# Weight preparation, gating and chunk decays issued in another order in a fused retention and SwiGLU kernel

## The chip, the cores and the metric

One Trainium2 chip, one core. The metric is device microseconds of one execution; lower is better. Three runs of the kernel before gave 822.98, 823.74 and 824.34 us.

## What is computed

A retention block feeds a SwiGLU feed-forward block. Queries, keys and values have shape (4, 8, 768, 64) in float32; the weights are (512, 1536), (512, 1536) and (1536, 512) and arrive as float64.

```python
for t in range(S):                                   # each batch and head
    state = gamma * state + outer(k[t], v[t])
    y[t] = q[t] @ state / sqrt(D)
x = y.transpose(0, 2, 1, 3).reshape(B * S, H * D)    # 3072 x 512
g = x @ w_gate
out = (g * sigmoid(g) * (x @ w_val)) @ w_out
```

## The kernel before

**Stages.** The 24 chunks of 128 positions (6 for each of 4 batches) are worked off in 4 segments of 6 chunks. The first stage is the retention of segment 0. Then, in each segment, `up` runs for 12 blocks f = 0 to 11 (columns of the two first weights), and `down` for 3 parts u. Between the products of `down` the steps of the next segment's retention are dealt out one by one, so that after the first stage retention has no stage of its own.

**Retention of a chunk.** `scores` multiplies k and q (PE) and masks the result out of PSUM (DVE); POOL makes a decayed copy of q (`qd`, L253) and of k (`kd`, L257). `mix` adds the old state's part and the masked part into the PSUM bank y, of which there is one, and ScalarE (ACT) copies it to xT. `state` multiplies `kd` with v and DVE scales the old state (L279) and adds (L280). After every second chunk DVE makes the sums `xs` (L334 to L337).

**A block of up.** Seven products, a Strassen-like scheme with 7 in place of 8, each of two float32 matmuls (four records in the profile), in this order: B11, T1, T2, B22, T3, B21, T4. B11, T2, T3 and T4 go through the bank x, T1 and B22 through w, B21 through z. ACT copies x after B11 (p, L359), w after T1 (p, L362) and x after T2 (u, L368); DVE adds after B22 (L370) and after T3 (L372), and adds z to the first copy (c, L377). ACT takes the silu of c (L378) and of x after T4 (sg, L381), and DVE multiplies both into hT (L382, L383). PE may not go on into a bank before it was read: T2 waits for the copy of L359, T3 for L368, T4 for the sum of L372.

**Weights.** In segment 0 each piece (12 `up`, 6 `down`) is turned from float64 words to float32: two ACT operations (`convert_a`), two tensor-scalar operations on DVE (`convert_b`), one combined operation on DVE (L188) and an integer add on POOL (L190). Then three operations make the sums that the scheme needs (L198 to L200): on POOL for `up`, on DVE for `down`. Finished `up` pieces are written to DRAM and read back in the later segments. There are three raw buffers, and the next load is issued on SP when a piece leaves its buffer. The table `at_block` says which pieces block f prepares: `up` f + 2, and in every even block the `down` piece f // 2 too.

**What sets the order.** Every engine runs its own instructions in the order in which the program issues them; nothing reorders them (`manual_schedule`). `retain(n)` issues n steps of the first retention, and `convert(f, 0)` and `convert(f, 1)` issue a block's preparation at two places in `up`. The list `late` holds the multiplications of a block, which are issued after T1 of the next.

Of the kernel before, what the change touches and what calls it, by code (L numbers as in the profile page):

```python
# [10 lines left out]
F32 = mybir.dt.float32  # L11
# [3 lines left out]
ALU = mybir.AluOpType  # L15
# [22 lines left out]
def tile_retnet_swiglu(  # L38
# [53 lines left out]

    def load_chunk(c, pool, tag):
        tiles = []
        for nm, src in (("kt", k_t), ("qt", q_t), ("kn", k_n), ("vn", v_n)):
            t = pool.tile([P, 512], F32, tag=nm + tag, name=f"{nm}_{c}")
            nc.sync.dma_start(out=t, in_=src[c])
            tiles.append(t)
        chunks[c] = tiles

# [81 lines left out]
    def convert_c(piece):  # L182

        kind, a = piece
        if piece in raw:
            w, d, lo, hi = words_of(piece)
            u = d.bitcast(U32)
            nc.vector.scalar_tensor_tensor(u, u, 3, hi, op0=ALU.logical_shift_left,  # L188
                                           op1=ALU.bitwise_xor)
            nc.gpsimd.tensor_tensor(d.bitcast(I32), u.bitcast(I32), lo.bitcast(I32),  # L190
                                    op=ALU.add)
            del raw[piece]
        w = wt[0, a] if kind == "up" else wot[a]
        sub = (nc.gpsimd if kind == "up" else nc.vector).tensor_tensor
# [6 lines left out]
        if kind == "up":  # L201
# [3 lines left out]

    at_block = [[("up", f + 2)] * (f + 2 < NF) + [("down", f // 2)] * (f % 2 == 0)
                for f in range(NF)]
    order = [("up", 0), ("up", 1)] + sum(at_block, [])
# [28 lines left out]
    def scores(c):  # L237
# [8 lines left out]
        for i in range(2):  # L246
            t = mid.tile([P, NP, P], F32, tag=f"a{i}", name=f"a{i}_{c}")
            nc.vector.tensor_tensor(t, pairs(sp[i]), mask[:, i], op=ALU.mult)  # L248
            a.append(t)
        att[c] = a  # L250
        if c % NCK:
            qd = mid.tile([P, NP, P], F32, tag="qd", name=f"qd_{c}", bufs=1)
            nc.gpsimd.tensor_tensor(qd, qt, qdec, op=ALU.mult)  # L253
            att[c, "qd"] = qd
        if c % NCK < NCK - 1:
            kd = mid.tile([P, H, D], F32, tag="kd", name=f"kd_{c}", bufs=1)
            nc.gpsimd.tensor_tensor(  # L257
                kd, chunks[c][2].rearrange("p (h d) -> p h d", h=H),
                kdec[:, :, None].to_broadcast([P, H, D]), op=ALU.mult)
            att[c, "kd"] = kd  # L260

    def state(c):
        ci = c % NCK
        if ci == NCK - 1:
            return
        kd = att.pop((c, "kd"))
        vn = chunks[c][3]
        st = bank("st", 1, f"st_{c}")
        for n in range(NP):
            nc.tensor.matmul(st[:, ts(n, P)], kd[:, ds(2 * n, 2)], vn[:, ts(n, P)],  # L270
                             start=(n == 0), stop=True, skip_group_check=True)
        new, old = state_of(c), state_of(c, 1)
        for i in range(2):
# [3 lines left out]
            else:  # L277
                g = gdec[r, :, None].to_broadcast([D, NP, D])
                nc.vector.tensor_tensor(new[r, :, r], old[r, :, r], g, op=ALU.mult)  # L279
                nc.vector.tensor_tensor(new[r, :, r], new[r, :, r],  # L280
                                        pairs(st)[r, :, r], op=ALU.add)

    def mix(c):
        ci = c % NCK
        vn = chunks[c][3]
        a = att.pop(c)
        y = bank("y", 1, f"y_{c}")
        if ci:
            qd = att.pop((c, "qd"))
            prev = state_of(c, 1)  # L290
# [50 lines left out]
    def up(s, f, convert):  # L341
# [20 lines left out]
        nc.scalar.copy(p5, wb)  # L362
        while late:
            late.pop(0)()
        convert(f, 0)
# [5 lines left out]
        product(x, T3, s3, start=False)  # L371
        tt(hT[:, f, 1], x, p5, op=add)  # L372
        convert(f, 1)
        z = bank("wz", 2, f"z_{s}_{f}")[:, :TH]
        product(z, B21, a_up(0, 1))
        c11 = tmp("c11", 2)
        tt(c11, z, p1, op=add)  # L377
        nc.scalar.activation(c11, c11, AF.Silu)  # L378
        product(x, T4, a_up(1, 1), start=False)
        sg = tmp("sg", 1)  # L380
        nc.scalar.activation(sg, x, AF.Silu)  # L381
        late.append(lambda: tt(hT[:, f, 0], hT[:, f, 0], c11, op=mul))  # L382
        late.append(lambda: tt(hT[:, f, 1], hT[:, f, 1], sg, op=mul))  # L383

# [63 lines left out]


    cs = seg_chunks(0)  # L450
    load_chunk(cs[0], first, "0")
    nc.scalar.dma_start(out=tab, in_=decays)
    for n in range(1, len(cs)):
        load_chunk(cs[n], first, str(n))
        if n in (2, 3, 4):
            load_next()
# [6 lines left out]

    retain(8)
    for p in order[:2]:
        convert_a(p)
        retain(2)
        convert_b(p)
        retain(2)
        convert_c(p)  # L470
        load_next()
    for p in at_block[0]:
        convert_a(p)
    retain(len(steps))
    early.__exit__(None, None, None)
    hp = ctx.enter_context(tc.tile_pool(name="hp", bufs=1))
    hT = hp.tile([P, NF, 2, TH], F32, name="hT")

    def convert(f, part):
        now = at_block[f]  # L480
        if part == 0:
            for p in now:
                convert_b(p)
            for p in now[:1]:
                convert_c(p)
                load_next()
        else:
            for p in now[1:]:
                convert_c(p)
                load_next()  # L490
            if f + 1 < NF:
                for p in at_block[f + 1]:
                    convert_a(p)

# [72 lines left out]
```

## Time and profile before

| what | value |
|---|---|
| median of 3 runs | 823.74 us |
| profiled execution | 824.35 us |
| its span, first to last instruction | 822.6 us |
| around the span | 1.75 us |
| PE (matmul) busy | 764.5 us, 93% of the span |
| DVE busy | 342.9 us, 42% |
| ACT busy | 190.7 us, 23% |
| POOL busy | 132.1 us, 16% |

A busy share is a mean over stages that are unlike each other; the rows further down tell the stages apart. Mean duration and idle time of a group of instructions stand in one row, with what ended the idle time.

### The profile page before, as it was taken

How to read it: one execution, taken by the hardware profiler on the slowest of the kernel's cores; microseconds unless marked ns; L12 is line 12 of the kernel's file. 1: busy time of each engine (PE TensorE's matmuls, PEld its weight loads, DVE VectorE, ACT ScalarE, POOL GpSimd, SP SyncE). 2: the span in 40 equal slices, each digit the busy share in tenths (PEclk: the TensorE clock that was granted, in tenths of full speed). 3: DMA queues.
4: the chain of work that ended last, by engine and by line, in shares of the span. 5: the costliest groups of instructions: out<-in, count | busy, mean ns of one | idle time of the engine just before them, and what ended most of it. 6: DMA issues, size and time to landing. Idle time of an engine off the chain costs nothing.

```text
span 822.6 us, 8808 instructions
## 1 busy us (share of the span) xinstructions
PE 764.5 (93%) x3440; PEld 535.8 (65%) x3440; DVE 342.9 (42%) x556; ACT 190.7 (23%) x358; POOL 132.1 (16%) x102
## 2 busy tenths in 40 slices
PE   6566779779999999999999999999999999999997
PEld 5443445445888755555888855555888855555886
DVE  3975555645536133233626333323555123322520
ACT  2333334432010123222110122222110122222100
POOL 3735556352111000000111100010111000000000
PEclk9978899889999999999999999999999999999999
DMA  9645655733245022340245022340254122220010
GB/s 335 209 147 180 210 174 179 229 126 117 90 167 180 26 90 100 124 147 1 90 167 179 27 89 90 112 169 0 69 188 146 59 90 90 89 90 0 1 41 37
DMA packets 40697, 95.74 MB, mean 116 GB/s; under 512 B 3664, under 2 KB 15952, under 8 KB 40656
## 3 DMA queue, kind: packets, MB, share of 16 engines
q1 hardware_dynamic: 37056, 88.09, 30.9%
q10 hardware_dynamic: 3600, 7.09, 2.5%
q8 instruction: 27, 0.44, 0.2%
q14 instruction: 14, 0.11, 0.0%
HBM read 77.86 MB, written 17.30 MB: 116 GB/s over the span
## 4 chain that ended last, share of the span: by engine, by line
PE 77%; DVE 1%; POOL 0%; ACT 0%; issue 0%; DVEq 0%; ACTq 0%; POOLq 0%
PE x L349 24%; PE dx L408 15%; PE w L349 12%; PE dw L408 8%; PE z L349 6%; PE dz L408 4%; PE s L243 2%; PE y L296 2%; PE y L292 2%; PE st L270 2%; POOL wot L190 0%; DVE wot L198 0%; DVE wot L188 0%; ACT sg L381 0%; DVE wot L199 0%
## 5 line engine op out<-in xcount | busy, mean ns | idle before, releaser
L349 PE MATMUL x<-xs,wt 128*128 128x384 f32 x384 | 147.3, 508 | 28.2 <-ACT p L359 28.2
L349 PE MATMUL w<-xs,wt 128*128 128x384 f32 x384 | 144.0, 499 | 0.6 <-DVE xs L334 0.6
L349 PE MATMUL x<-xT,wt 128*128 128x384 f32 x384 | 132.4, 486 | 1.1 <-DVE hT L372 1.1
L349 PEld LDWEIGHTS x<-xs,wt 128*128 128x128 f32 x384 | 75.8, 199 | 83.4 <-issue 35.2
L349 PEld LDWEIGHTS w<-xs,wt 128*128 128x128 f32 x384 | 75.3, 196 | 54.7 <-issue 5.2
L349 PEld LDWEIGHTS x<-xT,wt 128*128 128x128 f32 x384 | 72.8, 190 | 51.4 <-issue 1.7
L370 DVE TENSOR_TENSOR hT<-w,u 128x384 f32<-128x384 f32 x48 | 26.8, 558 | 168.9 <-PE w L349 163.0
L349 PE MATMUL z<-xT,wt 128*128 128x384 f32 x192 | 69.8, 486 | 0.0
L378 ACT ACTIVATE c<-c 128x384 f32<-128x384 f32 x48 | 25.1, 522 | 186.9 <-DVE c L377 186.9
L408 PE MATMUL dw<-wot,hs 128*128 128x256 f32 x288 | 67.3, 383 | 0.0
L253 POOL TENSOR_TENSOR qd<-qt,tab 128x512 f32<-128x512 f32 x20 | 27.4, 1369 | 247.8 <-PE y L292 120.5
L408 PE MATMUL dx<-wot,hs 128*128 128x256 f32 x288 | 67.0, 382 | 0.0
L408 PE MATMUL dx<-wot,hT 128*128 128x256 f32 x288 | 66.4, 381 | 0.0
L408 PEld LDWEIGHTS dw<-wot,hs 128*128 128x128 f32 x288 | 53.7, 190 | 8.7 <-issue 1.5
L408 PEld LDWEIGHTS dx<-wot,hT 128*128 128x128 f32 x288 | 53.7, 190 | 8.6 <-issue 1.0
L408 PEld LDWEIGHTS dx<-wot,hs 128*128 128x128 f32 x288 | 53.4, 190 | 7.7
L349 PEld LDWEIGHTS z<-xT,wt 128*128 128x128 f32 x192 | 36.5, 190 | 25.4
L257 POOL TENSOR_TENSOR kd<-kn,tab 128x512 f32<-128x512 f32 x20 | 21.9, 1093 | 187.1 <-DMA kn<-in_k_n_dram 96.5
L299 ACT COPY xT<-y 128x512 f32<-128x512 f32 x24 | 14.0, 584 | 150.3 <-PE y L296 150.2
L248 DVE TENSOR_TENSOR a<-s,tab 128x512 f32<-128x512 f32 x48 | 30.8, 684 | 40.6 <-PE s L243 40.6
L280 DVE TENSOR_TENSOR state<-state,st 64x256 f32<-64x256 f32 x32 | 13.4, 418 | 67.2 <-PE st L270 66.3
L243 PE MATMUL s<-qt,kt 64*128 64x128 f32 x384 | 30.3, 298 | 11.7 <-DMA qt<-in_q_t_dram 8.3
(58 smaller groups left out, 745.0 us busy)
## 6 DMA issues: line engine op xcount, KB each, us to landing
wt<-wstore SPq DMA_DIRECT2D x36, 896.0 KB, 4.6
wstore<-wt SPq DMA_DIRECT2D x12, 896.0 KB, 4.8
kt<-in_k_t_dram SPq DMA_DIRECT2D x24, 256.0 KB, 4.9
qt<-in_q_t_dram SPq DMA_DIRECT2D x24, 256.0 KB, 5.1
kn<-in_k_n_dram SPq DMA_DIRECT2D x24, 256.0 KB, 5.3
vn<-in_v_n_dram SPq DMA_DIRECT2D x24, 256.0 KB, 4.4
raw_up<-in_w_val_dram SPq DMA_DIRECT2D x24, 256.0 KB, 5.5
raw_up<-in_w_gate_dram SPq DMA_DIRECT2D x12, 512.0 KB, 6.0
```

The source lines that it names most:

```text
L243: nc.tensor.matmul(sp[i][:, ts(n, P)], kt[r, n], qt[r, n], start=True, stop=True, skip_group_check=True)
L248: nc.vector.tensor_tensor(t, pairs(sp[i]), mask[:, i], op=ALU.mult)
L253: nc.gpsimd.tensor_tensor(qd, qt, qdec, op=ALU.mult)
L257: nc.gpsimd.tensor_tensor(kd, chunks[c][2].rearrange("p (h d) -> p h d", h=H), kdec[:, :, None].to_broadcast([P, H, D]), op=ALU.mult)
L270: nc.tensor.matmul(st[:, ts(n, P)], kd[:, ds(2 * n, 2)], vn[:, ts(n, P)], start=(n == 0), stop=True, skip_group_check=True)
L292: nc.tensor.matmul(y[:, ts(n, P)], prev[:, n], qd[:, n], start=(n == 0), stop=False, skip_group_check=True)
L296: nc.tensor.matmul(y[ds(D * i, D), ts(n, P)], vn[:, ts(2 * n + i, D)], a[i][:, n], start=(ci == 0 and n == 0), stop=True, skip_group_check ...
L299: nc.scalar.copy(xT[:, :, c // NCK % 2, ts(ci % L, P)], pairs(y))
L349: nc.tensor.matmul(o, w[:, slot, k], a[:, k], start=(start and k == 0), stop=(stop and k == KH - 1), skip_group_check=True)
L370: tt(hT[:, f, 0], wb, u2, op=add)
L378: nc.scalar.activation(c11, c11, AF.Silu)
L408: nc.tensor.matmul(o, a[:, k], wot[k][:, slot], start=(start and k == 0), stop=(k == FH - 1), skip_group_check=True)
```

## The change

Six things change. (1) The three sums of a weight piece become a step of their own, `sums_t`. For the two pieces that the first stage converts, and for every `down` piece, it is issued later: at the start of the next block, from the list `due`. (2) The `down` pieces move from the even blocks to the odd ones (the last to block 10), and the first block's conversion is issued after the retention, not inside it. (3) The two silus of a block are issued on ACT after the second copy of the next block, and the two multiplications after that block's L372. (4) k and q are scaled in place, k first, where there were copies of their own. (5) The old state is scaled by ACT, in four operations of 128 columns, ahead of the products; DVE only adds. (6) The decay table is loaded in two parts on SP between the first chunk's tensors, v is loaded ahead of k, and the first weight piece is loaded one chunk earlier.

```diff
-        for nm, src in (("kt", k_t), ("qt", q_t), ("kn", k_n), ("vn", v_n)):
+        for nm, src in (("kt", k_t), ("qt", q_t), ("vn", v_n), ("kn", k_n)):
             t = pool.tile([P, 512], F32, tag=nm + tag, name=f"{nm}_{c}")
             nc.sync.dma_start(out=t, in_=src[c])
             tiles.append(t)
+            between(nm)
...
                                     op=ALU.add)
             del raw[piece]
+
+    def sums_t(piece):
+        kind, a = piece
         w = wt[0, a] if kind == "up" else wot[a]
         sub = (nc.gpsimd if kind == "up" else nc.vector).tensor_tensor
...
-    at_block = [[("up", f + 2)] * (f + 2 < NF) + [("down", f // 2)] * (f % 2 == 0)
-                for f in range(NF)]
+    at_block = [[("up", f + 2)] * (f + 2 < NF) + [("down", f // 2)] *
+                (f % 2 == 1 and f < NF - 1 or f == NF - 2) for f in range(NF)]
...
+        if c % NCK < NCK - 1:
+            kd = chunks[c][3].rearrange("p (h d) -> p h d", h=H)
+            nc.gpsimd.tensor_tensor(
+                kd, kd, kdec[:, :, None].to_broadcast([P, H, D]), op=ALU.mult)
         if c % NCK:
-            qd = mid.tile([P, NP, P], F32, tag="qd", name=f"qd_{c}", bufs=1)
-            nc.gpsimd.tensor_tensor(qd, qt, qdec, op=ALU.mult)
-            att[c, "qd"] = qd
-        if c % NCK < NCK - 1:
-            kd = mid.tile([P, H, D], F32, tag="kd", name=f"kd_{c}", bufs=1)
...
+            nc.gpsimd.tensor_tensor(qt, qt, qdec, op=ALU.mult)
...
+        if ci:
+            for n in range(NP):
+                nc.scalar.activation(new[:, n], old[:, n], AF.Copy,
+                                     scale=gdec[:, ds(n, 1)])
...
-                g = gdec[r, :, None].to_broadcast([D, NP, D])
-                nc.vector.tensor_tensor(new[r, :, r], old[r, :, r], g, op=ALU.mult)
                 nc.vector.tensor_tensor(new[r, :, r], new[r, :, r],
                                         pairs(st)[r, :, r], op=ALU.add)
...
         nc.scalar.copy(p5, wb)
-        while late:
-            late.pop(0)()
+        if late:
+            late[0]()
         convert(f, 0)
...
         tt(hT[:, f, 1], x, p5, op=add)
+        if late:
+            late.pop(0)
+            late.pop(0)()
         convert(f, 1)
...
-        nc.scalar.activation(c11, c11, AF.Silu)
...
-        nc.scalar.activation(sg, x, AF.Silu)
-        late.append(lambda: tt(hT[:, f, 0], hT[:, f, 0], c11, op=mul))
-        late.append(lambda: tt(hT[:, f, 1], hT[:, f, 1], sg, op=mul))
+
+        def gates():
+            nc.scalar.activation(c11, c11, AF.Silu)
+            nc.scalar.activation(sg, x, AF.Silu)
+
+        def muls():
+            tt(hT[:, f, 0], hT[:, f, 0], c11, op=mul)
+            tt(hT[:, f, 1], hT[:, f, 1], sg, op=mul)
+
+        late.extend([gates, muls])
...
+    def table(nm):
+        if nm == "qt":
+            nc.sync.dma_start(out=tab[:, :QDEC0], in_=decays[:, :QDEC0])
+        elif nm == "vn":
+            nc.sync.dma_start(out=tab[:, QDEC0:], in_=decays[:, QDEC0:])
+
     cs = seg_chunks(0)
-    load_chunk(cs[0], first, "0")
-    nc.scalar.dma_start(out=tab, in_=decays)
+    load_chunk(cs[0], first, "0", table)
...
-        if n in (2, 3, 4):
+        if n in (1, 3, 4):
             load_next()
...
-    for p in at_block[0]:
-        convert_a(p)
+    u0, u1 = order[:2]
+    retain(3)
+    convert_a(u0)
+    retain(3)
+    convert_b(u0)
+    retain(2)
+    convert_c(u0)
+    load_next()
+    convert_a(u1)
+    retain(3)
+    convert_b(u1)
+    retain(1)
+    sums_t(u0)
+    retain(4)
+    convert_c(u1)
+    load_next()
     retain(len(steps))
...
+    due = [u1]
+    for p in at_block[0]:
+        convert_a(p)
...
         if part == 0:
+            while due:
+                sums_t(due.pop(0))
             for p in now:
                 convert_b(p)
             for p in now[:1]:
                 convert_c(p)
                 load_next()
+                if p[0] == "up":
+                    sums_t(p)
+                else:
+                    due.append(p)
         else:
             for p in now[1:]:
                 convert_c(p)
                 load_next()
-            if f + 1 < NF:
-                for p in at_block[f + 1]:
-                    convert_a(p)
+                due.append(p)
+            for p in at_block[f + 1] if f + 1 < NF else []:
+                convert_a(p)
```

In the rows of the program's order below, line numbers of the change are those of its own file. The first place is DVE in block 2 of segment 0; `wot` is a `down` piece, `wt` an `up` piece, c the sum whose silu gates the block. Before:

```order
L178 TENSOR_SCALAR wt_4_477<-wt_4_477 128x1024
L180 TENSOR_SCALAR raw_up_478<-raw_up_478 128x1024
L178 TENSOR_SCALAR wot_94<-wot_94 128x1024
L180 TENSOR_SCALAR raw_down_497<-raw_down_497 128x1024
L188 SCALAR_TENSOR_TENSOR wt_4_477<-wt_4_477,raw_up_478 128x1024
L370 TENSOR_TENSOR hT<-w_2_564,u_0_2_592 128x384
L372 TENSOR_TENSOR hT<-x_2_563,p_0_2_571 128x384
L188 SCALAR_TENSOR_TENSOR wot_94<-wot_94,raw_down_497 128x1024
L198 TENSOR_TENSOR wot_94<-wot_94 128x2x256
L199 TENSOR_TENSOR wot_94<-wot_94 128x256
L200 TENSOR_TENSOR wot_94<-wot_94 128x256
L377 TENSOR_TENSOR c_0_2_615<-z_2_612,p_0_2_567 128x384
```

The same block of the change, from its first row on DVE:

```order
L201 TENSOR_TENSOR wot_93<-wot_93 128x2x256
L202 TENSOR_TENSOR wot_93<-wot_93 128x256
L203 TENSOR_TENSOR wot_93<-wot_93 128x256
L179 TENSOR_SCALAR wt_4_468<-wt_4_468 128x1024
L181 TENSOR_SCALAR raw_up_469<-raw_up_469 128x1024
L188 SCALAR_TENSOR_TENSOR wt_4_468<-wt_4_468,raw_up_469 128x1024
L370 TENSOR_TENSOR hT<-w_2_556,u_0_2_585 128x384
L372 TENSOR_TENSOR hT<-x_2_555,p_0_2_563 128x384
L389 TENSOR_TENSOR hT<-hT,c_0_1_550 128x384
L390 TENSOR_TENSOR hT<-hT,sg_1_554 128x384
L380 TENSOR_TENSOR c_0_2_602<-z_2_599,p_0_2_559 128x384
```

The sums of a `down` piece stood right ahead of c; now those of the piece of block 1 stand at the block's start, ahead of the sums that free the banks w and x (L370, L372).

The second place is ACT in the first stage, from the conversion of the second `up` piece to the first block. Before:

```order
L171 ACTIVATE wt_1_150<-raw_up_151 128x1024
L172 ACTIVATE raw_up_151<-raw_up_151 128x1024
L299 COPY xT<-y_340 128x4x128
L171 ACTIVATE wt_2_163<-raw_up_164 128x1024
L172 ACTIVATE raw_up_164<-raw_up_164 128x1024
L171 ACTIVATE wot_93<-raw_down_333 128x1024
L172 ACTIVATE raw_down_333<-raw_down_333 128x1024
L299 COPY xT<-y_402 128x4x128
L299 COPY xT<-y_425 128x4x128
L359 COPY p_0_0_461<-x_0_457 128x384
```

The same stretch of the change:

```order
L172 ACTIVATE wt_1_151<-raw_up_152 128x1024
L173 ACTIVATE raw_up_152<-raw_up_152 128x1024
L299 COPY xT<-y_290 128x4x128
L270 ACTIVATE state_100<-state_99,tab 128x128 x4
L299 COPY xT<-y_337 128x4x128
L270 ACTIVATE state_102<-state_101,tab 128x128 x4
L299 COPY xT<-y_389 128x4x128
L270 ACTIVATE state_99<-state_100,tab 128x128 x4
L299 COPY xT<-y_414 128x4x128
L270 ACTIVATE state_101<-state_102,tab 128x128 x4
L172 ACTIVATE wt_2_164<-raw_up_165 128x1024
L173 ACTIVATE raw_up_165<-raw_up_165 128x1024
```

The conversion of the first `down` piece no longer stands ahead of the last two copies to xT; the state scalings now stand between the copies, and one more copy stands behind the conversion of the second `up` piece.

## Rows read from the trace of the kernel before

**Rows 1.** Stages: length, busy PE, PEld, DVE, ACT, POOL, granted clock, DMA share, GB/s.

```profile
0.00:52.20 52.20, 28.26 (x272) 24.84 (x273) 31.48 (x39) 14.85 (x19) 26.52 (x26) 0.87 0.74 252
52.20:203.60 151.40, 121.53 (x339) 69.03 (x338) 85.28 (x131) 58.32 (x88) 72.06 (x48) 0.90 0.53 172
203.60:282.10 78.50, 78.50 (x526) 67.83 (x525) 37.45 (x63) 7.80 (x18) 9.48 (x8) 1.00 0.33 114
282.10:390.50 108.40, 108.40 (x338) 63.88 (x337) 32.49 (x59) 29.25 (x60) 1.04 (x1) 1.00 0.25 92
```

**Rows 2.** Costliest groups: shapes and count, busy us and mean ns, idle before and releaser.

```profile
L349 PE MATMUL x<-xs,wt 128*128 128x384 f32 x384 | 147.3, 508 | 28.2 <-ACT p L359 28.2
...
L378 ACT ACTIVATE c<-c 128x384 f32<-128x384 f32 x48 | 25.1, 522 | 186.9 <-DVE c L377 186.9
```

**Rows 3.** Timeline of blocks 2 and 3: start us, duration us, engine, instruction, idle.

```profile
90.83 2.37 POOL L190 TENSOR_TENSOR wot<-wot,raw_down 128x1024 int32<-128x1024 int32 x1
...
93.23 0.69 DVE L198 TENSOR_TENSOR wot<-wot 128x512 f32<-128x512 f32 x1 [5.11 <-POOL wot L190]
...
94.76 0.55 DVE L377 TENSOR_TENSOR c<-z,p 128x384 f32<-128x384 f32 x1
...
96.76 2.90 PE L349 MATMUL x<-xs,wt 128*128 128x384 f32 x4 [5.44 <-ACT p L359]
...
99.45 2.77 PE L349 MATMUL w<-xs,wt 128*128 128x384 f32 x4
```

**Rows 4.** Timeline, late in the first stage.

```profile
30.91 1.16 PE L243 MATMUL s<-qt,kt 64*128 64x128 f32 x16 [1.37 <-DMA qt<-in_q_t_dram]
...
44.77 1.13 ACT L171 ACTIVATE wot<-raw_down 128x1024 f32<-128x1024 f32 x1 [13.04 <-DMA raw_down<-in_w_out_dram]
...
47.53 2.05 PE L292 MATMUL y<-qd,state 128*128 128x128 f32 x8 [12.26 <-POOL wt L199]
```

**Rows 5.** Timeline, three places where DVE and POOL work at once.

```profile
31.04 2.58 POOL L190 TENSOR_TENSOR wt<-wt,raw_up 128x1024 int32<-128x1024 int32 x1
...
31.84 2.33 DVE L178 TENSOR_SCALAR wt<-wt 128x1024 f32<-128x1024 f32 x1
...
33.70 1.60 POOL L198 TENSOR_TENSOR wt<-wt 128x512 f32<-128x512 f32 x1
...
84.65 2.39 POOL L190 TENSOR_TENSOR wt<-wt,raw_up 128x1024 int32<-128x1024 int32 x1 [5.29 <-DVE wt L188]
...
84.98 0.56 DVE L370 TENSOR_TENSOR hT<-w,u 128x384 f32<-128x384 f32 x1 [0.55 <-PE w L349]
...
194.02 1.27 POOL L253 TENSOR_TENSOR qd<-qt,tab 128x512 f32<-128x512 f32 x1 [3.56 <-DMA qt<-in_q_t_dram]
194.09 1.61 DVE L382 TENSOR_TENSOR hT<-hT,c 128x384 f32<-128x384 f32 x1 [0.59 <-ACT c L378]
```

**Rows 6.** Timeline of block 1, such instructions with the other engine's port idle.

```profile
71.30 0.69 DVE L178 TENSOR_SCALAR wt<-wt 128x1024 f32<-128x1024 f32 x1
...
72.62 1.23 DVE L188 SCALAR_TENSOR_TENSOR wt<-wt,raw_up 128x1024 uint32<-128x1024 uint32 x1
...
76.47 1.28 POOL L198 TENSOR_TENSOR wt<-wt 128x512 f32<-128x512 f32 x1
...
77.83 0.73 POOL L199 TENSOR_TENSOR wt<-wt 128x256 f32<-128x256 f32 x1
```

**Rows 7.** Timeline of ACT and PE in blocks 0 and 2.

```profile
59.75 1.28 ACT L378 ACT_TABLE_LOAD   x1
...
82.38 0.48 ACT L362 COPY p<-w 128x384 f32<-128x384 f32 x1 [0.87 <-PE w L349]
...
83.67 0.48 ACT L368 COPY u<-x 128x384 f32<-128x384 f32 x1 [0.81 <-PE x L349]
...
84.71 1.45 PE L349 MATMUL x<-xs,wt 128*128 128x384 f32 x4
```

**Rows 8.** DMA issues: queue, count, KB each, median us from issue to landing.

```profile
qt<-in_q_t_dram SPq DMA_DIRECT2D x24, 256.0 KB, 5.1
```

More of the change, by code (lines that the diff above doesn't have):

```diff
@@ L91, in tile_retnet_swiglu, with load_chunk @@
     chunks = {}
-    def load_chunk(c, pool, tag):
+    def load_chunk(c, pool, tag, between=lambda nm: None):
         tiles = []
-        for nm, src in (("kt", k_t), ("qt", q_t), ("kn", k_n), ("vn", v_n)):
+        for nm, src in (("kt", k_t), ("qt", q_t), ("vn", v_n), ("kn", k_n)):
             t = pool.tile([P, 512], F32, tag=nm + tag, name=f"{nm}_{c}")
@@ L250, in scores @@
         att[c] = a
+        if c % NCK < NCK - 1:
+            kd = chunks[c][3].rearrange("p (h d) -> p h d", h=H)
+            nc.gpsimd.tensor_tensor(
+                kd, kd, kdec[:, :, None].to_broadcast([P, H, D]), op=ALU.mult)
         if c % NCK:
-            qd = mid.tile([P, NP, P], F32, tag="qd", name=f"qd_{c}", bufs=1)
-            nc.gpsimd.tensor_tensor(qd, qt, qdec, op=ALU.mult)
-            att[c, "qd"] = qd
-        if c % NCK < NCK - 1:
-            kd = mid.tile([P, H, D], F32, tag="kd", name=f"kd_{c}", bufs=1)
[L257 to L260, printed above, removed]
+            nc.gpsimd.tensor_tensor(qt, qt, qdec, op=ALU.mult)
     def state(c):
@@ L265, in state @@
             return
-        kd = att.pop((c, "kd"))
-        vn = chunks[c][3]
+        vn, kd = chunks[c][2:]
+        new, old = state_of(c), state_of(c, 1)
+        if ci:
+            for n in range(NP):
+                nc.scalar.activation(new[:, n], old[:, n], AF.Copy,
+                                     scale=gdec[:, ds(n, 1)])
         st = bank("st", 1, f"st_{c}")
         for n in range(NP):
-            nc.tensor.matmul(st[:, ts(n, P)], kd[:, ds(2 * n, 2)], vn[:, ts(n, P)],
+            nc.tensor.matmul(st[:, ts(n, P)], kd[:, ts(n, P)], vn[:, ts(n, P)],
                              start=(n == 0), stop=True, skip_group_check=True)
-        new, old = state_of(c), state_of(c, 1)
         for i in range(2):
@@ L284, in mix @@
         ci = c % NCK
-        vn = chunks[c][3]
+        qd, vn = pairs(chunks[c][1]), chunks[c][2]
         a = att.pop(c)
@@ L288, in mix @@
         if ci:
-            qd = att.pop((c, "qd"))
             prev = state_of(c, 1)
@@ L462, in retain @@
                 steps.pop(0)()
-    retain(8)
-    for p in order[:2]:
-        convert_a(p)
[L467 to L471, printed above, removed]
-    for p in at_block[0]:
-        convert_a(p)
+    u0, u1 = order[:2]
[14 more added lines that the diff above has]
+    load_next()
     retain(len(steps))
@@ L490, in convert @@
                 load_next()
-            if f + 1 < NF:
-                for p in at_block[f + 1]:
-                    convert_a(p)
+                due.append(p)
+            for p in at_block[f + 1] if f + 1 < NF else []:
+                convert_a(p)
     for s in range(NSEG):
```

## Prediction

> **What bounds the kernel now.** The profiled execution took 824.35 us, 0.6 over the median: a span of 822.6 and 1.75 around it. I read the busy time by stage first. From 203.6 us on PE is busy for the whole of its stages, 78.5 of 78.5 and 108.4 of 108.4 us, at a granted clock of 1.00 [rows 1]. Only its own work counts there, and the change takes none away. A block of `up` is 108.4 / 12 = 9.03 us, a product 1.29. What can be had lies ahead of that: in the first stage PE is busy for 28.3 of 52.2 us, and segment 0's `up` takes 151.4 us where twelve such blocks would take 108.4.
>
> Next the costliest groups. The matmuls that follow T1 were idle for 28.2 us in all, ended by ACT's copy of x (L359), and the silu of c waited 186.9 us for DVE [rows 2]. The timeline shows the link. POOL finishes the integer add of a `down` piece at 93.20; DVE had its sum L198 at the head of the queue for 5.11 us, so c comes at 94.76. Both silus and the copy are behind c on ACT, and T2 starts at 96.76, after 5.44 us idle [rows 3]. T2 and the next product then take 2.69 (to 99.45) and about 2.6 us in place of 1.29: PE is back on the lower of its two clock levels (the stage's mean is 0.90, [rows 1]). A wait thus costs 5.4 + 2.7, and a pair of blocks lasts 18.06 + 8.1 = 26.2 us.
>
> In the first stage PE is idle for 12.26 us before 47.53. The row names POOL, but ACT is the cause: it held the first `down` piece's conversion for 13.04 us, until the load landed at 44.77, with the copy to xT behind it, and y has one bank [rows 4].
>
> **The port.** What DVE and POOL cost each other decides this forecast. Alone, a `convert_b` operation takes 0.69, L188 1.23, and POOL's sums 1.28 and 0.73 [rows 6]. Under POOL's integer add, which ends at 33.62, DVE's L178 lasts until 34.17, 0.55 past it, and POOL's next sum takes 1.60 in place of 1.28. A multiplication begun at 194.09 ends at 195.70, 0.41 after POOL's operation. But the sum L370, which reads PSUM, takes 0.56 under the add at 84.65 [rows 5]. So DVE operations whose inputs are all in SBUF take turns with POOL's, and those with a PSUM input do not.
>
> The Trainium skill (SBUF — State Buffer, "Who interferes with whom") says that the loser of this pair "fully blocks" and that the winner holds it for the whole instruction. By it the turns would be dearer than the rows show, which is a rival below.
>
> **The change, first stage.** The 12.26 us wait goes: the `down` conversion stands behind the retention. The last chunk still lands at 30.91, since about the same bytes come ahead of it. From there PE needs scores 1.16, then two mixes and states of about 3.4, to 38.9 [rows 4]: the floor. Next late is the port. From the first piece's integer add on, POOL has that add (2.4), six scalings (1.27 for one of q [rows 5], taken at 1.15 each, 6.9), three sums (2.7), and between them six DVE operations (taken at 0.4 each, 2.3): 14.3 us. The add began at 31.04 [rows 5]; its piece is now loaded one chunk earlier and it stands ahead of four of the scalings, so I take 23.8. The last q is then scaled at 38.1, the last mask follows at about 39.2, y and state end at 42.6. Ends: 38.9, and 46 if the add starts half as early. Gain 52.2 - 42.6 = 9.6. The table in two parts starts the first scores sooner, hidden by the load of the last chunk. Without that cover it is at most a landing, 5.1 us [rows 8], as a gain.
>
> **The change, blocks of segment 0.** The two `down` steps now lie in two blocks, so I walk a pair. Time 0 is the end of a `down` piece's add; DVE, at the head of an even block, waits for it. Sums to 1.53 (93.23 to 94.76, [rows 3]). Two `convert_b` (1.32, from 71.30 to 72.62, [rows 6]) and L188 to 4.1. POOL's add 4.3 to 6.7. DVE's L370 and L372 read PSUM and end at 5.1, so PE starts T4 at 5.2. First multiplication 6.7 + 0.41 = 7.1; POOL's sum, held, to 8.25; second multiplication 8.7; sum to 9.25; c 9.2; then the odd block's first `convert_b` 9.8, POOL's last sum 10.4, second `convert_b` 10.9, and two more and L188 with POOL idle, to 13.4. The odd block's `up` add 13.6 to 16.0, with L370 and L372 under it to 14.4. Multiplication 16.4, sum 17.5, multiplication 17.9, sum 18.5, L188 of the `down` piece 19.6, sum 20.1, its add 20.2 to 22.6, the next time 0.
>
> So a pair takes 22.6 us in place of 26.2. PE, which needs 18.06, waits about 4.3 before T4 of the even block and 0.3 in the odd one. DVE and POOL set the pace, so slow products after such a wait, up to 2.7 us as in [rows 3], mostly fit into the next: DVE needs T3 at 13.8 and PE has 0.7 to spare. I add nothing, at most 0.4 a pair.
>
> The first pair: block 0 takes 9.9 (the last sums `xs` are late), its c ends at 9.4, the odd part of the walk takes 13.5 (9.1 to 22.6), and T3 of block 1 is 1.8 late, of which 0.95 is the table load below: the first time 0 is 24.7 after the start. Then four pairs, 90.4; 5.2 to T4 and 1.29 for it; block 11, whose sums meet an idle POOL, 9.03. Sum 130.6 against 151.4: gain 20.8.
>
> **The change, ScalarE.** In a free block the second copy ends at 82.86, the third starts at 83.67 and ends at 84.15, T3 starts at 84.71 [rows 7]: 0.81 + 0.56 = 1.37 to spare, and two silus at 0.52 [rows 2] need 1.04. They fit in all 48 blocks. Only in block 1 the table load (1.28, [rows 7]) stands with them: 2.32 - 1.37 = 0.95 late, once.
>
> The Trainium skill (ScalarE: Activation LUTs, "What ACT_TABLE_LOAD costs") gives such a switch another 1.38 us for a drain; by it the sum would be 795.3. No row here shows the drain: the load stands in idle time.
>
> The trace has no scaling of 128 columns: above nothing and below the copy of 384 columns, 0.48 [rows 7], so 0 to 1.9 a chunk. I take 1.1, from the copy's columns; ACT is idle for most of the later stages, and in the first it runs beside the port's queue. The 32 DVE multiplications that go (L279) lie under PE's full stages, but for eight in the first stage; there the walk has left them out.
>
> **The change, loads.** In place, a q buffer comes free after its mix and not after its copy. Two or three products of `down` lie between that and the scores that need the next chunk, so I cost it at nothing; with that cover gone, each of 12 such loads would show a landing of up to 5.1 us [rows 8]. Deferred sums on POOL for the second piece end well ahead of block 1.
>
> **Sum.** 824.35 - 9.6 - 20.8 = 793.95, so 794.
>
> **Rivals.** *DVE and POOL do not take turns.* For: L370 ran freely [rows 5]. Against: the two other places there. Alone, the loop is 1.5 + 2.6 + 2.5 + 2.6 + 1.2 + 0.2 on DVE and 2.4 + 3.0 + 2.4 on POOL, 18.4: four pairs save 16.8, the first 2, giving 775. Chance 0.10.
>
> *The port is held for the full durations.* Three adds at 2.39, two sets of sums at 2.74, six `convert_b` at 0.69, three L188 at 1.23, four multiplications at 0.56 and 1.53 make 24.2 a pair: 4 x 1.6 more, 800. Against: 0.55 and 0.41 above are shorter than 0.69 and 0.56. Chance 0.14. This is what the rule of the Trainium skill (SBUF — State Buffer, "Who interferes with whom") comes to here.
>
> *The wait moves to a load.* The next `down` piece is loaded into the buffer that time 0 frees; its conversion (2 x 1.13, [rows 4]) stands on ACT ahead of the odd block's first copy, which T2 needs at about 9.1. With a landing of 5 to 6 us it ends at 8.3. From 1 us later each us lengthens the pair by as much; 3.6 later, pairs last 26.2 as now, and the time is 808. For: 13.04 us were waited for such a load [rows 4]. Chance 0.14.
>
> *Slower: the silus come between the second and third copy of every block.* Where they need over 1.37 us, T3 waits 48 times. To eat up 30.4 us each pair of silus would need 2.0, 0.63 over the spare; with a table load in every block it would be 2.3, and the time about 840. Against: one load stands between Copy and Silu in the whole trace [rows 7]. Chance 0.04.
>
> **How the numbers follow.** The forecast has 0.57, no change 0.01. Its own range is 786 to 803: pairs of 21.5 to 24 us, a first stage of 38.9 to 46. For 8 in 10 it must take in the late load and the full durations, and of the rest little: 782 to 810. A measurement here tells 0.2% (1.6 us) from nothing. Faster: 0.57 + 0.10 + 0.14 + 0.14 = 0.95; within 0.2% 0.01; slower 0.04.
>
> **What would show it.** Block 0 starts near 42.6 and the 12 us wait is gone. T2's waits are gone; in even blocks PE is idle for about 4 us before T4, ended by DVE's L372. Multiplications under POOL's work last 1.5 to 2 us in segment 0 and 0.56 later. The stages after it keep 78.5 and 108.4. It is wrong if those grow, if PE waits for a copy on ACT, or if pairs are near 18 or 26 us.

## Result and profile after the change

The changed kernel takes 796.38 us (median of four runs, 794.46 to 796.97), the kernel before in the same session 824.04: a ratio of 0.966, 95% interval 0.9639 to 0.9681. Forecast were 794.0 and 782 to 810. The profiled execution took 796.35 us, a span of 794.6 and 1.75 around it.

The stages of the changed kernel, columns as in [rows 1]; the second row is `up` of segment 0, the third the first `down`, the last the third `down`:

```profile
0.00:41.80 41.80, 28.66 (x272) 25.24 (x273) 20.90 (x32) 15.10 (x32) 20.97 (x23) 0.92 0.84 293
41.80:172.20 130.40, 114.35 (x338) 64.55 (x337) 109.02 (x130) 61.98 (x92) 79.03 (x51) 0.97 0.60 207
172.20:253.00 80.80, 78.91 (x525) 67.99 (x524) 33.92 (x56) 12.92 (x35) 12.21 (x9) 1.00 0.32 111
...
548.10:627.40 79.30, 78.90 (x525) 67.97 (x524) 32.79 (x55) 12.67 (x35) 12.45 (x9) 1.00 0.33 114
```

Against [rows 1] the first stage lost 10.4 us and segment 0's `up` 21.0. The first `down` grew from 78.4 to 80.8 (between the first products of the stages, where [rows 1] round to 78.5) and the third from 78.4 to 79.3, together 3.4 us, which nothing in the forecast allows for. All other stages are as long as before.

Two of the costliest groups hold T4 and T3 of all blocks. In [rows 2] the matmuls behind T1 had waited 28.2 us for ACT's copy. That wait is gone, and 13.9 us of waiting for DVE's sum L372 stand ahead of T4:

```profile
L349 PE MATMUL x<-xT,wt 128*128 128x384 f32 x384 | 136.3, 497 | 13.9 <-DVE hT L372 13.9
L349 PE MATMUL x<-xs,wt 128*128 128x384 f32 x384 | 139.8, 487 | 1.2 <-ACT u L368 1.2
```

The timeline of one even block, the place that answers to [rows 3], from the end of a `down` piece's add to the next such end:

```profile
89.17 0.69 DVE L201 TENSOR_TENSOR wot<-wot 128x512 f32<-128x512 f32 x1 [2.50 <-POOL wot L190]
...
93.47 2.39 POOL L190 TENSOR_TENSOR wt<-wt,raw_up 128x1024 int32<-128x1024 int32 x1 [4.33 <-DMA raw_down<-in_w_out_dram]
93.63 0.55 DVE L372 TENSOR_TENSOR hT<-x,p 128x384 f32<-128x384 f32 x1
94.10 2.17 DVE L389 TENSOR_TENSOR hT<-hT,c 128x384 f32<-128x384 f32 x1
94.33 4.51 PE L349 MATMUL x<-xT,wt 128*128 128x384 f32 x8 [3.46 <-DVE hT L372]
95.08 1.15 ACT L172 ACTIVATE wot<-raw_down 128x1024 f32<-128x1024 f32 x1 [4.27 <-DMA raw_down<-in_w_out_dram]
95.94 1.48 POOL L201 TENSOR_TENSOR wt<-wt 128x512 f32<-128x512 f32 x1
96.20 1.64 DVE L390 TENSOR_TENSOR hT<-hT,sg 128x384 f32<-128x384 f32 x1
...
111.67 0.69 DVE L201 TENSOR_TENSOR wot<-wot 128x512 f32<-128x512 f32 x1 [2.51 <-POOL wot L190]
```

Read it in three steps. The two rows of L201 are 22.5 us apart: a pair of blocks. Both multiplications stretch under POOL's work, from 0.55 alone (at 173.70) to 2.17 and 1.64, while L372, which reads PSUM, takes 0.55 under the same add. And PE's T4 waits 3.46 for L372, because DVE reaches it that late. (POOL's wait of 4.33 is put down to a DMA; but DVE's L188, whose result this add needs, ends only at 93.25.) Both sorts of wait fit one queue, that of DVE and POOL together; e1 and e2 test it.

### The profile page after: what moved, and what is told of

It reads as the page before. It is cut to its first block, busy times and chain, and to the rows that moved or that the text cites. A ratio compares the mean times of both kernels' runs of the same rounds, so it can differ in the third digit from the quotient of the medians.

```text
span 794.6 us, 8792 instructions
## 1 busy us (share of the span) xinstructions
PE 758.9 (96%) x3440; PEld 532.4 (67%) x3440; DVE 333.4 (42%) x524; ACT 202.4 (25%) x422; POOL 138.2 (17%) x102
## 4 chain that ended last, share of the span: by engine, by line
PE 77%; DVE 3%; issue 0%; ACT 0%; DVEq 0%; ACTq 0%
PE x L349 24%; PE dx L417 15%; PE w L349 12%; PE dw L417 7%; PE z L349 6%; PE dz L417 4%; PE y L296 2%; PE s L246 2%; PE y L292 2%; PE st L274 2%; DVE hs L407 1%; DVE hT L390 0%; DVE a L251 0%; DVE hT L372 0%; DVE wot L201 0%
## 5 line engine op out<-in xcount | busy, mean ns | idle before, releaser
L349 PE MATMUL x<-xT,wt 128*128 128x384 f32 x384 | 136.3, 497 | 13.9 <-DVE hT L372 13.9
L349 PE MATMUL x<-xs,wt 128*128 128x384 f32 x384 | 139.8, 487 | 1.2 <-ACT u L368 1.2
L349 PE MATMUL w<-xs,wt 128*128 128x384 f32 x384 | 139.6, 486 | 0.9 <-DVE xs L334 0.9
L370 DVE TENSOR_TENSOR hT<-w,u 128x384 f32<-128x384 f32 x48 | 26.7, 557 | 214.0 <-PE w L349 213.1
L349 PEld LDWEIGHTS x<-xs,wt 128*128 128x128 f32 x384 | 72.7, 190 | 53.2 <-ACT u L368 3.3
L349 PEld LDWEIGHTS w<-xs,wt 128*128 128x128 f32 x384 | 73.0, 190 | 52.4 <-DVE xs L334 1.6
L257 POOL TENSOR_TENSOR kn<-kn,tab 128x512 f32<-128x512 f32 x20 | 25.2, 1261 | 330.4 <-DMA kn<-in_k_n_dram 330.4
L359 ACT COPY p<-x 128x384 f32<-128x384 f32 x48 | 23.0, 479 | 226.2 <-PE x L349 226.1
L251 DVE TENSOR_TENSOR a<-s,tab 128x512 f32<-128x512 f32 x48 | 30.9, 684 | 44.8 <-PE s L246 44.8
L260 POOL TENSOR_TENSOR qt<-qt,tab 128x512 f32<-128x512 f32 x20 | 26.6, 1331 | 91.2 <-PE s L246 56.3
```

What stands on the lines that cost most here:

```text
L257: nc.gpsimd.tensor_tensor(kd, kd, kdec[:, :, None].to_broadcast([P, H, D]), op=ALU.mult)
L260: nc.gpsimd.tensor_tensor(qt, qt, qdec, op=ALU.mult)
L349: nc.tensor.matmul(o, w[:, slot, k], a[:, k], start=(start and k == 0), stop=(stop and k == KH - 1), skip_group_check=True)
L359: nc.scalar.copy(p1, x)
L370: tt(hT[:, f, 0], wb, u2, op=add)
```

## Experiments

Each edit is made in the changed kernel, unless another is named. Times are medians, and ratios stand to the kernel before of the same session.

**e1: the multiplications read PSUM.**

```diff
-        z = bank("wz", 2, f"z_{s}_{f}")[:, :TH]
+        z = bank(("y", "st")[f % 2], 1, f"z_{s}_{f}")[:, :TH]
         product(z, B21, a_up(0, 1))
-        c11 = tmp("c11", 2)
-        tt(c11, z, p1, op=add)
+        tt(z, z, p1, op=add)
...
-            nc.scalar.activation(c11, c11, AF.Silu)
-            nc.scalar.activation(sg, x, AF.Silu)
+            nc.scalar.activation(z, z, AF.Silu)
+            nc.scalar.activation(x, x, AF.Silu)
...
-            tt(hT[:, f, 0], hT[:, f, 0], c11, op=mul)
-            tt(hT[:, f, 1], hT[:, f, 1], sg, op=mul)
+            tt(hT[:, f, 0], hT[:, f, 0], z, op=mul)
+            tt(hT[:, f, 1], hT[:, f, 1], x, op=mul)
```

> c and the second silu stay in PSUM (z in the banks of y and st in turn, x in its own), so that both multiplications read PSUM. Turns at the port: the two multiplications of a block need no turn any more and take about 0.56 us under POOL's work; by the walk the pair is 21.3 to 21.6 in place of 22.5, about 1 us less in each of five pairs: 791, range 789 to 793. If the next down piece's load sets the pace of the pair, it stays 22.5 and the time 796 to 797. If the port is held for full durations, the pair loses two full turns, 2 x 0.56 twice: 786 to 788.

Measured 789.64 us, ratio 0.9582 (0.9562 to 0.9601). The timeline of the same block:

```profile
88.83 0.69 DVE L201 TENSOR_TENSOR wot<-wot 128x512 f32<-128x512 f32 x1 [4.63 <-POOL wot L190]
...
93.12 2.39 POOL L190 TENSOR_TENSOR wt<-wt,raw_up 128x1024 int32<-128x1024 int32 x1 [4.33 <-DMA raw_down<-in_w_out_dram]
93.29 0.55 DVE L372 TENSOR_TENSOR hT<-x,p 128x384 f32<-128x384 f32 x1
93.75 0.54 DVE L387 TENSOR_TENSOR hT<-hT,z 128x384 f32<-128x384 f32 x1
...
94.22 0.54 DVE L388 TENSOR_TENSOR hT<-hT,x 128x384 f32<-128x384 f32 x1
...
110.08 0.69 DVE L201 TENSOR_TENSOR wot<-wot 128x512 f32<-128x512 f32 x1 [3.30 <-POOL wot L190]
```

The same two multiplications, in the same place under the same add, with one operand moved to PSUM: 0.54 us in place of 2.17 and 1.64. The pair is 21.25. Turns at the port are shown; a pace set by a load is not what held it at 22.5. Of the profiled time, `up` of segment 0 gives 5.9 us and the first `down` 1.6, and the first stage, whose instructions are the same, is 1.7 longer.

**e2: more work for POOL where it idles.**

```diff
-        sub(w[:, T2], w[:, B22], w[:, T1], op=ALU.subtract)
-        sub(w[:, T4], w[:, B21], w[:, T2], op=ALU.subtract)
+        for _ in range(3 if kind == "up" and a and a % 2 == 0 else 1):
+            sub(w[:, T2], w[:, B22], w[:, T1], op=ALU.subtract)
+            sub(w[:, T4], w[:, B21], w[:, T2], op=ALU.subtract)
```

> POOL repeats two sums of each even up piece twice (four more operations of 0.73 us, 2.9 us), at a place where by the walk it idles for about 3 us while DVE works on SBUF alone. Turns at the port: DVE gets its operations only between them and each costs it 0.5 to 0.7 us; pair 22.5 + 2.0 to 2.9, five pairs: 806 to 811, taken at 808.5. Engines that do not hinder each other, or a pace set by the load of the down piece: the operations fall into POOL's idle time, 796 to 798.

Measured 805.98, ratio 0.978 (0.9765 to 0.9794). From the timeline of an odd block, DVE's conversions and POOL's added sums (lines 203 and 204 here):

```profile
104.44 1.22 DVE L181 TENSOR_SCALAR raw_up<-raw_up 128x1024 uint32<-128x1024 uint32 x1
105.19 1.06 POOL L203 TENSOR_TENSOR wt<-wt 128x256 f32<-128x256 f32 x1
105.58 1.22 DVE L179 TENSOR_SCALAR wot<-wot 128x1024 f32<-128x1024 f32 x1
106.33 1.06 POOL L204 TENSOR_TENSOR wt<-wt 128x256 f32<-128x256 f32 x1
```

They alternate strictly, 1.22 in place of 0.69 and 1.06 in place of 0.73 [rows 6]. Pairs are 24.4 us: four added operations cost 1.9, 0.48 each, a little under the 0.5 expected at least, and the time is just under the range.

**e3, e4 and e5: the two parts of the change in the blocks, back one at a time and together.** e3 puts the silus right behind c and T4 and both multiplications ahead of the next block's conversions:

```diff
         tt(c11, z, p1, op=add)
+        nc.scalar.activation(c11, c11, AF.Silu)
         product(x, T4, a_up(1, 1), start=False)
         sg = tmp("sg", 1)
-        def gates():
...
+        nc.scalar.activation(sg, x, AF.Silu)
...
-        late.extend([gates, muls])
+        late.append(muls)
```

> The silus and multiplications alone go back to where they were. If moving them is what the blocks of segment 0 gained from, about 20 us come back: 812 to 817. By the walk the pace belongs to DVE's and POOL's turns: the copy of x waits behind a late c and both silus again and T2 of even blocks waits 3 to 4 us, but in place of T4; the first multiplication at a block's head costs 1 to 2 us a pair: 800 to 806, taken at 803.

Measured 799.10, ratio 0.9697 (0.9679 to 0.9715): 2.7 us over the changed kernel, just below the range. Pairs are 23.1; T2 waits only 0.4, in two blocks, since c no longer stands behind a `down` sum; T4 goes on waiting, 2.0 to 3.4. The expected wait of T2 in place of T4 did not come.

e4 puts the conversions and sums of pieces in their old order:

```diff
-    at_block = [[("up", f + 2)] * (f + 2 < NF) + [("down", f // 2)] *
-                (f % 2 == 1 and f < NF - 1 or f == NF - 2) for f in range(NF)]
+    at_block = [[("up", f + 2)] * (f + 2 < NF) + [("down", f // 2)] *
+                (f % 2 == 0) for f in range(NF)]
...
                 load_next()
-                due.append(p)
+                sums_t(p)
```

> The order of conversions alone goes back: both pieces in even blocks, the down sums right behind POOL's add. If the deferred sums are what the blocks gained from, about 20 us come back: 812 to 817. By the walk the same operations take the same turns, DVE waits for the down add in the even block instead of the next one, and the late c stands behind no copy that T2 needs, only the third: pair 22.5 to 23.5, 796 to 802, taken at 798.

Measured 801.52, ratio 0.9726 (0.9708 to 0.9745), within the range and 5.1 over the changed kernel. c is late again, but of the copies only the third stands behind it: T3 waits 2.9 to 4.6, and DVE goes on with conversions. Pairs are 22.95. e5 has both edits.

> Both go back together: silus and multiplications to their old place, and the old order of conversions with the sums at once. If the two parts earn their gains independently, the losses of e3 and e4 add: 796.4 + 2.7 + 5.1 = 804, 803 to 806. If each part alone breaks the one chain (the late c with both silus ahead of the copy that T2 needs), the chain returns only now: pair 26.2 as before, 3.7 more in each of five pairs: 815, 813 to 818. I take the second.

Measured 818.66, ratio 0.9928 (0.991 to 0.9946). The timeline shows the chain of [rows 3] back, link by link:

```profile
83.36 2.37 POOL L190 TENSOR_TENSOR wot<-wot,raw_down 128x1024 int32<-128x1024 int32 x1
85.76 0.69 DVE L201 TENSOR_TENSOR wot<-wot 128x512 f32<-128x512 f32 x1 [5.09 <-POOL wot L190]
...
87.88 0.52 ACT L378 ACTIVATE c<-c 128x384 f32<-128x384 f32 x1 [9.11 <-DVE c L377]
...
88.67 0.47 ACT L359 COPY p<-x 128x384 f32<-128x384 f32 x1
...
89.29 2.90 PE L349 MATMUL x<-xs,wt 128*128 128x384 f32 x4 [5.45 <-ACT p L359]
```

T2 waits 5.45 us, pairs take 25.3 to 26.8 us, and `up` of segment 0 takes 152.9, no less than before the change. The time is a little above the range. Alone the edits lose 2.7 and 5.1, together 22.3. Either part alone breaks the chain: the deferred sums where POOL's add holds up c, the later silus where c holds up the copy. So the 21.0 us that `up` of segment 0 gained can be credited to neither.

**e6: the scaled q in a buffer of its own.**

```diff
-            nc.gpsimd.tensor_tensor(qt, qt, qdec, op=ALU.mult)
+            qd = mid.tile([P, NP, P], F32, tag="qd", name=f"qd_{c}", bufs=1)
+            nc.gpsimd.tensor_tensor(qd, qt, qdec, op=ALU.mult)
+            att[c, "qd"] = qd
...
```

> The scaled q of a chunk goes to a buffer of its own again; k stays scaled in place. If the 3.4 us that the later segments lost come from q's scaling, which in place must wait for the scores and then takes turns with DVE's sums of h: 3.0 less, 793.4, range 792.5 to 794.5, and the first part of down after segment 0 takes 78.4 to 78.8 in place of 80.8. If they come from the silus, which stand 0.7 us later at the end of up and push those sums back: 795.5 to 797, that part still 80 or more.

First the changed kernel, at the start of its first `down`:

```profile
170.71 1.05 POOL L257 TENSOR_TENSOR kn<-kn,tab 128x512 f32<-128x512 f32 x1 [7.46 <-DMA kn<-in_k_n_dram]
170.77 1.40 DVE L390 TENSOR_TENSOR hT<-hT,sg 128x384 f32<-128x384 f32 x1
...
172.21 2.75 PE L417 MATMUL dx<-wot,hT 128*128 128x256 f32 x12
...
176.17 1.27 POOL L260 TENSOR_TENSOR qt<-qt,tab 128x512 f32<-128x512 f32 x1 [4.42 <-PE s L246]
176.28 1.98 DVE L407 TENSOR_TENSOR hs<-hT,hs 128x768 f32<-128x768 f32 x1
177.40 1.76 POOL L257 TENSOR_TENSOR kn<-kn,tab 128x512 f32<-128x512 f32 x1
178.18 1.79 DVE L407 TENSOR_TENSOR hs<-hT 128x768 f32<-128x768 f32 x1
...
180.62 1.75 PE L246 MATMUL s<-qt,kt 64*128 64x128 f32 x16 [1.78 <-DVE a L251]
```

q is scaled over itself, so POOL must wait for the scores that read it; the next k stands behind it. Both then fall on DVE's sums of h, which take 1.98 and 1.79 in place of 0.96. The masks (L251) come late and PE waits 1.78; the scores behind take 1.75 in place of 1.16. A turn under k's first scaling (L390, 1.40) has pushed those sums back before that: they start 2.08 us after the first product of `down`, where before the change it was 1.38. In e6:

```profile
170.50 1.27 POOL L261 TENSOR_TENSOR qd<-qt,tab 128x512 f32<-128x512 f32 x1
...
172.11 1.04 POOL L257 TENSOR_TENSOR kn<-kn,tab 128x512 f32<-128x512 f32 x1 [0.34 <-DMA kn<-in_k_n_dram]
...
174.58 2.75 PE L420 MATMUL dx<-wot,hT 128*128 128x256 f32 x12
...
179.01 0.95 DVE L410 TENSOR_TENSOR hs<-hT 128x768 f32<-128x768 f32 x1
...
181.14 1.23 PE L246 MATMUL s<-qt,kt 64*128 64x128 f32 x16
```

Both scalings run before `down` begins, the last sum of h takes 0.95, and PE does not wait. This `down` takes 78.4 us, as expected of q's scaling. But its sums of h also start earlier here, 1.57 after its first product. The clean case is the third `down`: the sums start at 1.38 in both kernels, and it takes 78.4 in e6 where the changed kernel's takes 79.3. Late silus alone don't explain the loss: the third `down` of the changed kernel and the first of e4 and of e8 (below) have them too, their sums start at 1.38 all the same, as before the change, and these stages take 79.3. So the turns with q and the next k cost 0.9 in each of two stages. The late start that L390's turn makes adds 1.5 in the first, since q's scaling then holds the third sum too: in e1, whose multiplications take no turns, the sums start at 1.29 and the stage takes 79.2. What such a start costs with q apart, no run shows.

The time is 795.42, ratio 0.9646 (0.963 to 0.9662), which can't be told from the changed kernel's, and above the range. The trace shows where the gain of the later stages went. The first stage ended 0.7 us later (42.50), and its first add had started 0.8 later; this need not be the edit's work, since e1, e2 and e3, which leave that stage as it is, start the add up to 1.9 later. And `up` of segment 0 took 132.1 in place of 130.4: its last T4 starts after a wait of 3.46, and it and the product behind it take 4.51 at a granted clock of 0.62, where the changed kernel's waits 2.49 and takes 2.82.

**e7: e4 with the first `down` piece converted ahead of the last two mixes.**

```diff
     convert_c(u1)
     load_next()
+    for p in at_block[0]:
+        convert_a(p)
     retain(len(steps))
...
     sums_t(u1)
-    for p in at_block[0]:
-        convert_a(p)
```

> The kernel of e4 with one more step back: the first down piece is converted ahead of the last two mixes again. If that place alone made the 12.26 us wait, it returns: 8 to 10 over e4, 810 to 812. If the wait hung on when the piece's load could start, which the earlier conversion of the first up piece has moved forward by 10 us, the load has landed by about 36: first stage up to 2 us longer, 801 to 804, taken at 803.

Measured 802.07, ratio 0.9722 (0.9708 to 0.9736), 0.5 over e4. ACT's timeline has no wait at the place where [rows 4] show 13.04 us:

```profile
26.65 3.25 SPq L153 DMA_DIRECT2D raw_down<-in_w_out_dram  x4
...
36.45 1.14 ACT L172 ACTIVATE wot<-raw_down 128x1024 f32<-128x1024 f32 x1
```

The place of the conversion was not the cause. What differs is when the piece's load is issued: here right behind the first `up` piece's add, which ends at 26.63 and frees the raw buffer. In the kernel before that add ended at 33.62 [rows 5], and the load stood on SP behind the store of the piece's three sums:

```profile
37.31 0.33 SPq L202 DMA_DIRECT2D wstore<-wt  x1
37.75 2.70 SPq L152 DMA_DIRECT2D raw_down<-in_w_out_dram  x4
```

Of the 11.1 us between the two issues, 7.0 are thus the earlier add and 4.1 the deferred sums with their store. No run has one without the other.

**e8: the old state scaled by DVE.**

```diff
-        if ci:
-            for n in range(NP):
-                nc.scalar.activation(new[:, n], old[:, n], AF.Copy,
-                                     scale=gdec[:, ds(n, 1)])
...
+                g = gdec[r, :, None].to_broadcast([D, NP, D])
+                nc.vector.tensor_tensor(new[r, :, r], old[r, :, r], g, op=ALU.mult)
```

> The old state is scaled by DVE again. In the later stages nothing. In the first stage eight more operations of 0.41 us on SBUF alone, in the port's queue with POOL: 0 to 3.3 us, taken at 1.6: 798.0, range 796.4 to 799.7.

Measured 798.55, ratio 0.9692 (0.967 to 0.9713). In the first stage one such scaling is held by POOL's add, and PE's next product for the state waits until DVE's add behind that scaling (L279, to 44.28) has read the one bank st:

```profile
41.08 2.46 POOL L190 TENSOR_TENSOR wt<-wt,raw_up 128x1024 int32<-128x1024 int32 x1 [3.20 <-issue]
...
41.80 2.02 DVE L278 TENSOR_TENSOR state<-state,tab 64x256 f32<-64x256 f32 x1
...
44.38 2.05 PE L270 MATMUL st<-vn,kn 128*128 128x128 f32 x8 [3.43 <-issue]
```

Block 0 starts at 46.23, 22.3 us after the first add, where in the changed kernel it is 18.5: 3.7 more, which is over the expected 0 to 3.3. The time is within its range because two other stages are shorter: `up` of segment 0 by 1.1, so that `down` begins at 175.52, 3.3 later, and the first `down` by 1.5 (79.3), where the sums of h start 0.7 earlier. That the total came out near 798.0 is in part luck.

**e9, e10, e11: three steps on from e1.** e9 has four raw buffers in place of three and one load more ahead.

> The kernel of e1 with a fourth raw buffer, and one load more issued ahead. If turns at the port set the pace, the loads are earlier and nothing else: pair 21.2, 789 to 791. If the loads set it, the pair falls to 18 to 20: 778 to 786.

Measured 790.17, ratio 0.9585 (0.9571 to 0.9599); pairs 21.15. Earlier loads alone bring nothing.

e10 has e1 with the `down` sums behind c:

```diff
-            while due:
-                sums_t(due.pop(0))
+            if f % 2 or not f:
+                settle()
...
         tt(z, z, p1, op=add)
+        if s == 0 and f % 2 == 0:
+            settle()
```

(`settle` does what the two lines did.)

> The kernel of e1 with the down sums behind c of the even block, and no longer at its head, where DVE waits 3.3 to 4.6 us for POOL's add. If that wait costs the pair its length, 1 to 1.5 us a pair: 782 to 785. But the up piece that DVE would take up instead is on ACT until 1.0 us behind the end of that add, since its load lands late, and the sums meet POOL's elsewhere: at most 0.3 a pair, 788 to 790. I take the second.

Measured 784.35, ratio 0.9518 (0.95 to 0.9536), against what I took. The premise of what I took does not hold in e1's trace: the `up` piece that DVE takes up there leaves ACT at 82.75, 6.0 us ahead of the end of the `down` add at 88.79; the one that leaves it later, at 91.15, belongs to the next block. So DVE can start on it while POOL adds, and in e10 it does, at 84.88 under an add that ends at 87.00. No T4 waits any more. What is late next is the load: in two of the blocks ACT waits for a piece with the copy that T2 needs behind it, and T2 waits 1.94 and 4.01:

```profile
115.35 1.17 ACT L172 ACTIVATE wot<-raw_down 128x1024 f32<-128x1024 f32 x1 [5.11 <-DMA raw_down<-in_w_out_dram]
...
118.04 2.90 PE L349 MATMUL x<-xs,wt 128*128 128x384 f32 x4 [4.01 <-ACT p L359]
```

e11 has e9 and e10 together, and from segment 1 on a buffer for the scaled q.

> e9 and e10 together, and the scaled q in a buffer of its own from segment 1 on, where there is room once the raw buffers are gone. With early loads DVE can take up the next piece while POOL adds the last: pair 20.0 to 20.5, 5 x 0.9 = 4.5 less than e1, and 1.8 in the later segments: 783.5, 781 to 786. If the sums pay at their new place what they saved at the old: 787 to 788.5.

Measured 777.84, ratio 0.9436 (0.942 to 0.9451), below the range and well under both kernels. Pairs are 19.7. The stage of segment 0's `up`:

```profile
41.70:157.00 115.30, 109.56 (x338) 63.38 (x337) 106.94 (x130) 61.30 (x92) 84.36 (x52) 1.00 0.65 224
```

It is 6.9 us over the 108.4 of twelve full blocks, where the changed kernel's is 22.0. Its first `down` takes 78.9 and its third 78.4, where e10's each take 79.25. The fourth buffer, worth nothing in e9, takes away the waits of T2 that e10 had left; T4 waits 1.4 in three of the pairs.

## Why the prediction was right, and where not

**The sum.** 793.95 was forecast. The first stage ended 0.8 earlier, `up` of segment 0 took 0.2 less, and the later stages 3.4 more: 796.35, the profiled time. The forecast was right in two of three terms; the growth of the later stages was costed at nothing.

**First stage.** The walk along the port held. The first add starts at 23.27 (taken 23.8), the last q is scaled by 36.4 (38.1), the last mask ends at 38.8 (39.2), block 0 starts at 41.80 (42.6). From the first add to block 0 that is 18.5 us (18.8), and 18.3 to 18.6 in e1, e2 and e3, which have the same first stage. The start of the add was an estimate, and it moves: in these three it comes at 24.6 to 25.2. That the stage came out within 0.8 is luck to that extent. And the reason given for the vanished 12.26 us, that the conversion now stands behind the retention, is wrong by e7; what counts is that the load is issued 11 us earlier, since the first piece is added earlier and its sums are put off. Which of the other moves in this stage earned how much of the 10.4 us, the runs don't separate, but for the state scaling (e8).

**Blocks of segment 0.** The pair of 22.6 (measured 22.5), the first time 0 at 24.7 (24.9) and the 130.6 (130.4) came out of turns at the port, and e1 and e2 show that these turns set the pace. The length of the pair is not luck, for the walk holds step by step: counted from the add's end at 89.13, L188 ends at 4.1, the `up` add at 6.7, the two multiplications at 7.1 and 8.7, c at 9.2, the odd block's `up` add at 15.9, its multiplications at 16.4 and 17.9, and the next `down` add at 22.5, all within 0.1 of it. Only the odd block's L372 ends later, at 15.5 in place of 14.4, since it waits for T3, and no product waits for it. The wait ahead of T4 is 2.0 in the first pair and then 3.46 and 2.5 us by turns, not 4.3: each wait of 3.46 is followed by slow products, which shorten the next. The silus fit: T3 waits 0.3 in two odd blocks of segment 0. In block 1 it waits 0.62 for the table load, not 0.95.

**Rivals.** *DVE and POOL do not take turns* (775) falls with e1 and e2. *The port held for full durations* (800): L389 begins at 94.10 under an add that ends at 95.86 and is done 0.41 later, not 0.55. Summed over a pair, such differences make 22.5 and not 24.2. The Trainium skill (SBUF — State Buffer, "Who interferes with whom") says that the winner has the shared ports for its whole instruction and the loser is fully blocked. The trace agrees as far as L389 ends only behind the add; but 0.14 of its 0.55 us is gone by then, so that its full duration overstates the turn. *The wait moves to a load* (808): ACT does wait 4.27 for the `down` piece, but DVE takes its result up only later. It became true in e10, when the turns had been shortened. *The silus late in every block* (840) did not occur: one table load, and T3 waits 1.2 us in all.

The Trainium skill (ScalarE: Activation LUTs, "What ACT_TABLE_LOAD costs") adds a drain of 1.38 us to a table switch. Here the load stands between a copy that ends at 55.35 and a silu, with work waiting:

```profile
55.37 1.28 ACT L385 ACT_TABLE_LOAD   x1
...
56.66 0.53 ACT L385 ACTIVATE c<-c 128x384 f32<-128x384 f32 x1
```

The load starts 0.02 us behind the copy's end and the silu 0.01 behind the load's; no drain shows.

**The step that failed** is "in place [...] I cost it at nothing", and with it that the stages after 203.6 keep 78.5 and 108.4; by the sign that the forecast names itself (wrong if those grow) it failed here, with 3.4 us measured. I looked at when q's buffer comes free for the next load, and there nothing waits. I did not look at what q's scaling itself must wait for: the scores that read the same buffer. Before, it ran at 194.02 in the last blocks of `up`, ahead of `down`; in place it runs when DVE makes the sums of h, and both read SBUF alone. That is the same rule of turns that I had used in segment 0, not applied to a later stage. e6 shows it for the first `down` (80.8 to 78.4) and the third (79.3 to 78.4), though its whole time did not fall by as much. Of the 3.4, 1.9 are these turns in both stages, and 1.5 come on top in the first, where the sums of h start late because L390 takes a turn with the scaling of k.

**State scaling.** Taken at 1.1 us a chunk on ACT, measured 1.28 for four operations. That it takes eight operations out of the port's queue is worth 3.7 in the first stage (e8), but only 2.2 in the whole time.

## What to carry to other kernels

Where two engines share a port, add up their turns over the repeating unit and lay them along both queues in order; that gave the length of a pair to 0.1 us here (22.6, measured 22.5), where the same walk without turns gives 18.4 us. An operand left in PSUM takes its operation out of that queue, here at no price (0.54 us against 0.55 alone): e1 gained 6.7 us by it without a single instruction less. And a buffer saved by working in place turns every reader of the old value into a wait: ask when the operation will now run, and beside what. When a load is late, look too at what stands ahead of it on its queue: here it was a store that waited for three sums.

## What the runs showed of the hardware

The clock's fall after a wait does not follow from the wait's length alone. In the changed kernel T4 and the product behind it took 4.51 us after both waits of 3.46 and 2.82 after those of 2.50 and 2.49, and the granted clock of the two stretches (columns as in [rows 1]) was 0.63 and 1.00, part of the first at the lower level of 1.2 GHz:

```profile
94.30:98.90 4.60, 4.57 (x9) 2.62 (x10) 4.60 (x5) 2.19 (x3) 4.36 (x4) 0.63 0.39 119
...
116.80:119.70 2.90, 2.88 (x9) 1.81 (x10) 2.90 (x2) 2.23 (x3) 2.82 (x2) 1.00 0.09 15
```

But e1 has two waits of 2.87 ahead of the same product, one followed by 4.51 us and one by 2.82:

```profile
93.98 4.51 PE L349 MATMUL x<-xT,wt 128*128 128x384 f32 x8 [2.87 <-DVE hT L372]
...
136.41 2.82 PE L349 MATMUL x<-xT,wt 128*128 128x384 f32 x8 [2.87 <-DVE hT L372]
```

What decides between them stays open. Where such a loss falls matters more than whether it does: in the middle of segment 0 the next wait absorbs most of it; ahead of the last blocks it is paid in full, which in e6 is 1.7 of the 2.4 us by which it came late to `down`.
